# Chunked attention and a gated FFN on one core: weight blocks of 1024 columns, a new plan, and score and value products that take either half of two PSUM banks

## The chip, the cores and the metric

The kernel runs on one NeuronCore of a Trainium2 chip. The metric is device microseconds of one execution; the time of a kernel is the median of its runs. TensorE (PE in the profile) does the matrix products, VectorE (DVE) and ScalarE (ACT) the element-wise work, GpSimd (POOL) some element-wise work on SBUF, and SyncE (SP) issues all DMAs in one queue, in order.

## The reference

```python
q_c, k_c, v_c = (a.reshape(B, H, S // 64, 64, D) for a in (q, k, v))   # B, H, S, D = 8, 8, 576, 64
scores = np.matmul(q_c, k_c.transpose(0, 1, 2, 4, 3)) / np.sqrt(D)
attn = np.exp(scores - scores.max(-1, keepdims=True))
attn = attn / (attn.sum(-1, keepdims=True) + 1e-9)
x = np.matmul(attn, v_c)             # to (B, S, H * D), d_model = 512
h = np.maximum(x @ w_in, 0.0)        # d_ff = 1024
conv_out = sum of conv_w[k] * h shifted by k - 1 along S, k = 0, 1, 2
out = (h / (1 + np.exp(-conv_out))) @ w_out
```

The activations are float32; the weights `w_in`, `conv_w`, `w_out` arrive as float64 and are read as pairs of 32-bit words.

## The kernel before

The 4608 rows of the batch are cut two ways: 36 tiles of 128 rows (two attention chunks of 64 each) for the attention and the output, and 16 units of 288 columns for the FFN, of which each has 8 blocks of 128 features.

**Attention, per tile** (`att`, L436). The first nine tiles load q and k as rows (`load_rows`, L98, two DMAs of 256 KB, into one of six slots), transpose them on TensorE (`t_pe`, L139) and copy them out on ScalarE. The other tiles come in groups of three by `load_group` and `load_part` (L108 to L126), eight parts to a group, two group buffers, and are transposed on VectorE (`t_dve`, L150, from line 153). Then: `scores` (L155, 16 small matmuls, line 163), `s_max` and `s_sub` on VectorE (L173, L177), exp on ScalarE (L182), sum and reciprocal on VectorE, the normalisation on GpSimd (L195), a transpose on TensorE (L202), a copy (L207), `attn_v` (L209, 16 small matmuls, line 215), and the split of x in a high and a low fp32r part, `x_hi` on ScalarE (L239) and `x_lo` on VectorE (L243). v has five buffers. The PSUM tile `sx` is a pair of banks that scores and attn @ v share: scores always write columns 0 to 255 of both banks, attn @ v columns 256 to 511.

**Weights** (`split`, L401). A block of a weight matrix is 128 partitions by 512 float64 numbers. It lands in one of the same six slots and is turned into a high and a low fp32r matrix by steps on VectorE: `w_mask` (L334), `w_rest` (L343), `w_low` (L347), `w_sign` (L352), `w_pow` (L369); `w_bias` (L339) and the copies `w_hi`, `w_lo_copy` (L362, L380) on ScalarE; `w_lo_big` (L377) on GpSimd. In every second block (`hi_pool`) `w_one` (L358) and a product on GpSimd, `w_hi_one` (L365), take the place of `w_sign` and `w_hi`. There are eight blocks of `w_in`, eight of `w_out` and one small one of `conv_w`.

**FFN.** A block of a unit is `mm1` (L246, 12 matmuls of 290 columns on line 252 into one of three `h_ps` banks), then relu and the convolution on ScalarE and VectorE (L258 to L281), whose last step `c_mul` (L281) frees the `h_ps` bank, then `g_hi` (L290, ScalarE) and `g_lo` (L294, GpSimd). `mm2` (L299, line 305) takes three matmuls of 512 columns per tile and feature block, eight of these to an output tile; `o_copy` (L310) takes the result to one of three `o_sb` buffers and `o_store` (L313) to memory.

**What sets the order.** All steps are listed with an engine, a cost, a key and the buffers that they take and free (`step`, L66; `room`, L397). A planner (L595 to L684) lays them out by these costs and by keys that tables shift (`by_step`, `by_chain`, L566 to L583), and the instructions of each engine are then held to that order. A step with `bank="sx"` is planned so that it doesn't run while another engine works in the pair of banks.

Of the kernel before, what the change touches and what calls it, by code (L numbers as in the profile page):

```python
# [30 lines left out]
def attn_ffn(ctx: ExitStack, tc: tile.TileContext, q, k, v, w_in, conv_w, w_out, out):  # L31
    nc = tc.nc
# [14 lines left out]
    NU = 2 * B  # L47
    NAT = 9
# [29 lines left out]
    rebias = const.tile([P, 1], F32, name="rebias")  # L78
    nc.gpsimd.memset(rebias, -896.0 * 2 ** 23)
# [16 lines left out]
    slots = [sp[:, 1024 * i:1024 * i + 1024] for sp in spare for i in range(TG)]  # L96

    def load_rows(st, t):  # L98
        r = slots[st["slot"]].rearrange("p (i c) -> p i c", i=2)
# [39 lines left out]
    def t_pe(st, i):  # L139

        st["tp", i] = tp = ps_h.tile([P, 512], F32, name="h_ps")
        rows = slots[st["slot"]][:, 512 * i:512 * i + 512]
        for g in range(G):
            nc.tensor.transpose(out=tp[:, P * g:P * g + P], in_=rows[:, P * g:P * g + P], identity=ident)  # L144
# [9 lines left out]

    def scores(st):  # L155

        s_ps = sx[:, :, 0:G * C]
# [12 lines left out]
    def s_max(st):  # L170
        st["sv"] = sx[:, :, 0:G * C].rearrange("p u (g j) -> p u g j", j=C)
# [37 lines left out]
    def attn_v(st):  # L209
        x_ps = sx[:, :, G * C:2 * G * C]  # L210
# [97 lines left out]
    def o_copy(st):  # L308
        st["os"] = work3.tile([P, DM], F32, name="o_sb")
# [9 lines left out]
    def w_load(st, src):  # L319
        np_, n, m2 = src.shape  # L320
        t = slots[st["slot"]].bitcast(U32)[0:np_, 0:n * m2].rearrange("p (n m) -> p n m", m=m2)
# [5 lines left out]
    def w_tile(st, name):  # L327
        t = (work3 if name == "o_sb" else work).tile([P, DM], F32, name=name)
# [3 lines left out]
    def w_mask(st):  # L332
        st["T"] = w_tile(st, "o_sb")
# [21 lines left out]
    def w_one(st):  # L355

        st["S"] = w_tile(st, "ws")
        nc.vector.tensor_scalar(out=st["S"].bitcast(U32), in0=st["H"], scalar1=0x80000000, scalar2=0x3F800000,  # L358
                                op0=ALU.bitwise_and, op1=ALU.bitwise_or)

# [3 lines left out]
    def w_hi_one(st, hi):  # L364
        nc.gpsimd.tensor_tensor(out=hi, in0=st["T"], in1=st["S"], op=ALU.mult)  # L365

    def w_pow(st, hi):
        st["E"] = w_tile(st, "we")
        nc.vector.tensor_scalar(  # L369
            out=st["E"].bitcast(U32), in0=(st["T"] if hi is None else hi).bitcast(U32), scalar1=0xFF800000, scalar2=None,  # L370
# [30 lines left out]
    def split(key, t_load, src, hi=None, lo=None, hi_pool=False, lo_pool=False, lag=1.5):  # L401
# [34 lines left out]
    def att(t, key, load_key, exps, writes):  # L436
# [16 lines left out]
        ldv = step("SP", 2.65, load_key + 0.05 if t < 5 else key - 8, load_v, (st, t), [before.get("v")], take=["v"], lag=1.28)  # L453
# [4 lines left out]
        s = step("DVE", 0.68, key, s_sub, (st,), [s], take=["e"], free=["m", "s"], bank="sx")  # L458
# [25 lines left out]
    def block(key, u, f, after):  # L484
# [4 lines left out]
        s = step("ACT", 0.5, key + 2, c_mid, (st, u, f), [s, cw_done], take=["c"])  # L489
# [26 lines left out]
    def wi(n, key, t_load, **kw):  # L516

        ks = slice(2 * (n % 2), 2 * (n % 2) + 2)
        ends = split(key, t_load, src_i[n], wi_h[:, n // 2, ks, :], wi_l[:, n // 2, ks, :], lag=1.5, **kw)
        for f in (n - n % 2, n - n % 2 + 1):  # L520
            wi_done[f] = wi_done.get(f, []) + list(ends)

    def wo(f, key, t_load, **kw):
# [195 lines left out]
```

## Time and profile before

| | us |
|---|---|
| median of 3 runs | 533.53 (531.76 to 535.38) |
| the profiled execution | 533.55 |
| its span, first to last instruction | 531.8 |
| TensorE busy in the span | 500.3 |
| VectorE busy | 364.6 |
| ScalarE busy | 359.4 |
| GpSimd busy | 184.9 |

The profile shows one execution. Busy times are shares of the span; a wait is the idle time of an engine just before an instruction, put down to what released it last. An average over the span says little here, because the first 90 us and the rest have different limits: stretches have to be read apart.

### The profile page before, as it was taken

The numbers are of one execution on the slowest core, as the hardware profiler recorded it, in microseconds if no ns is written. First come the engines' busy times: TensorE is split into PE (matmuls) and PEld (weight loads), VectorE is DVE, ScalarE is ACT, GpSimd is POOL, SyncE is SP. The second block draws the span as 40 slices with busy tenths as digits, with TensorE's granted clock in tenths as the row PEclk, the third lists the DMA queues.
The fourth block names the chain that finished last, engine by engine and source line by source line (L and its number), as shares of the span: only waits on it lengthen the run. The fifth ranks groups of instructions, "written<-read, shape, count | busy, mean of one in ns | idle before, by whom it ended". The sixth has DMA issues, their size and how long they took to land.

```text
span 531.8 us, 12836 instructions
## 1 busy us (share of the span) xinstructions
PE 500.3 (94%) x4921; PEld 437.6 (82%) x4921; DVE 364.6 (69%) x763; ACT 359.4 (68%) x818; POOL 184.9 (35%) x250
## 2 busy tenths in 40 slices
PE   3577889999999999999989999999999999999997
PEld 2467777988889898889878888889889889988975
DVE  6878999848668775866668586869756597554420
ACT  3568898857766868656756868767666578775630
POOL 2346757531423424322413324231334324241320
PEclk9988998999999999999999999999999999999999
DMA  8996581453344555333644643335440020000011
GB/s 207 241 235 179 129 185 39 108 96 62 48 94 90 105 107 105 87 64 64 109 110 87 128 75 62 64 82 110 78 95 24 21 62 2 21 21 21 21 48 52
DMA packets 183266, 47.03 MB, mean 88 GB/s; under 512 B 175500, under 2 KB 175524, under 8 KB 183204
## 3 DMA queue, kind: packets, MB, share of 16 engines
q1 hardware_dynamic: 183204, 46.20, 39.1%
q8 instruction: 39, 0.64, 0.5%
q14 instruction: 23, 0.19, 0.1%
HBM read 36.72 MB, written 9.44 MB: 87 GB/s over the span
## 4 chain that ended last, share of the span: by engine, by line
PE 78%; SPq 7%; DVE 6%; ACT 5%; DMA 3%; issue 1%; POOL 0%; ACTq 0%; DVEq 0%; POOLq 0%
PE o_ps L305 34%; PE h_ps L252 34%; SPq L124 4%; PE sx_ps L215 3%; PE sx_ps L163 3%; PE pt_ps L202 3%; PE h_ps L144 1%; SPq L136 1%; DMA qk<-in_moe_w_in 1%; DMA v<-in_v 1%; ACT c L263 1%; DVE c L267 1%; ACT L278 1%; DVE c L281 1%; DVE c L273 1%
## 5 line engine op out<-in xcount | busy, mean ns | idle before, releaser
L294 POOL TENSOR_TENSOR g_l<-c,g_h 128x288 fp32r<-128x288 f32 (+8 forms) x184 | 113.5, 633 | 231.7 <-ACT g_h L290 221.6
L305 PE MATMUL o_ps<-wo_h,g_h 128*128 128x512 f32 x288 | 116.9, 406 | 0.6 <-ACT wo_h L362 0.6
L305 PE MATMUL o_ps<-wo_l,g_h 128*128 128x512 f32 x288 | 113.9, 395 | 2.3 <-ACT wo_l L380 2.2
L305 PE MATMUL o_ps<-wo_h,g_l 128*128 128x512 f32 x288 | 113.9, 395 | 0.0
L267 DVE SCALAR_TENSOR_TENSOR c<-h_ps,cw,c 128x288 f32<-128x288 f32 (+1 forms) x128 | 65.6, 513 | 62.3 <-ACT c L263 61.4
L252 PE MATMUL h_ps<-x_h,wi_h 128*128 128x290 f32 x512 | 94.1, 307 | 4.5 <-DVE c L281 4.2
L252 PE MATMUL h_ps<-x_l,wi_h 128*128 128x290 f32 x512 | 91.3, 301 | 0.0
L252 PEld LDWEIGHTS h_ps<-x_h,wi_h 128*128 128x128 f32 x512 | 79.8, 192 | 13.8 <-DVE c L281 6.9
L252 PE MATMUL h_ps<-x_h,wi_l 128*128 128x290 f32 x512 | 90.5, 299 | 0.0
L278 ACT ACTIVATE c<-c 128x288 f32<-128x288 f32 x128 | 55.8, 443 | 38.1 <-DVE c L273 37.0
L252 PEld LDWEIGHTS h_ps<-x_l,wi_h 128*128 128x128 f32 x512 | 77.5, 193 | 0.0
L252 PEld LDWEIGHTS h_ps<-x_h,wi_l 128*128 128x128 f32 x512 | 77.2, 192 | 0.0
L281 DVE TENSOR_TENSOR c<-h_ps,c 128x288 f32<-128x288 f32 x128 | 56.9, 452 | 27.6 <-ACT c L278 26.2
L290 ACT CAST g_h<-c 128x288 fp32r<-128x288 f32 (+8 forms) x184 | 59.4, 357 | 19.9 <-DVE c L281 16.0
L258 ACT ACTIVATE h_ps<-h_ps 128x290 f32<-128x290 f32 x128 | 50.9, 398 | 29.6 <-PE h_ps L252 28.9
L263 ACT ACTIVATE c<-h_ps,cw 128x288 f32<-128x288 f32 x128 | 63.8, 500 | 9.9 <-POOL g_l L294 2.2
L273 DVE SCALAR_TENSOR_TENSOR c<-h_ps,cw,c 128x288 f32<-128x288 f32 (+1 forms) x128 | 65.7, 515 | 3.5
L305 PEld LDWEIGHTS o_ps<-wo_h,g_l 128*128 128x128 f32 x288 | 54.2, 188 | 12.4 <-POOL g_l L294 0.2
L305 PEld LDWEIGHTS o_ps<-wo_l,g_h 128*128 128x128 f32 x288 | 54.3, 188 | 11.0 <-ACT wo_l L380 3.2
L305 PEld LDWEIGHTS o_ps<-wo_h,g_h 128*128 128x128 f32 x288 | 54.3, 189 | 10.4 <-ACT wo_h L362 0.8
L195 POOL TENSOR_TENSOR e<-e,z 128x512 f32<-128x512 f32 x36 | 39.3, 1092 | 64.5 <-DVE z L192 56.4
L310 ACT COPY o_sb<-o_ps 128x512 f32<-128x512 f32 x36 | 21.0, 584 | 33.0 <-PE o_ps L305 32.4
(53 smaller groups left out, 536.0 us busy)
## 6 DMA issues: line engine op xcount, KB each, us to landing
v<-in_v SPq DMA_DIRECT2D x144, 64.0 KB, 2.8
out<-o_sb SPq DMA_DIRECT2D x36, 256.0 KB, 2.1
qk<-in_q SPq DMA_DIRECT2D x96, 48.0 KB, 2.4
qk<-in_k SPq DMA_DIRECT2D x96, 48.0 KB, 2.2
qk<-in_moe_w_in SPq DMA_DIRECT2D x8, 512.0 KB, 6.5
qk<-in_moe_w_out SPq DMA_DIRECT2D x8, 512.0 KB, 5.5
qk<-in_q SPq DMA_DIRECT2D x96, 24.0 KB, 1.9
qk<-in_k SPq DMA_DIRECT2D x96, 24.0 KB, 1.9
```

Source lines behind the costliest of these rows:

```text
L124: nc.sync.dma_start(out=groups[j][p0:p0 + 32, i, g, n0:n0 + 2 * n, :], in_=(q, k)[i][b, 2 * g + hp, t0:t0 + C * n, 32 * a:32 * a + 32].rea ...
L195: nc.gpsimd.tensor_tensor(out=st["e"], in0=st["e"], in1=st["z"].rearrange("p (h o) -> p h o", o=1).broadcast_to([P, H, C]), op=ALU.mult)
L252: nc.tensor.matmul(h_ps[:, 0:XU], lhsT=wt[:, f // 2, kt, P * (f % 2):P * (f % 2) + P], rhs=xt[:, u % NX, kt, :], start=n == 0, stop=n == 3 ...
L258: nc.scalar.activation(out=st["h"][:, 0:XU], in_=st["h"][:, 0:XU], func=AF.Relu)
L263: nc.scalar.mul(out=st["c"], in_=st["h"][:, i0:i0 + HS], mul=cw[:, FT + f:FT + f + 1])
L267: nc.vector.scalar_tensor_tensor(out=c[:, a:HS], in0=st["h"][:, i0 + a - 1:i0 + HS - 1], scalar=cw[:, f:f + 1], in1=c[:, a:HS], op0=ALU.mu ...
L273: nc.vector.scalar_tensor_tensor(out=c[:, 0:b], in0=st["h"][:, i0 + 1:i0 + 1 + b], scalar=cw[:, 2 * FT + f:2 * FT + f + 1], in1=c[:, 0:b], ...
L278: nc.scalar.activation(out=st["c"], in_=st["c"], func=AF.Sigmoid)
L281: nc.vector.tensor_tensor(out=st["c"], in0=st["h"][:, st["i0"]:st["i0"] + HS], in1=st["c"], op=ALU.mult)
L290: nc.scalar.copy(out=g_h[:, f, gs], in_=st["c"][:, cs])
L294: nc.gpsimd.tensor_tensor(out=g_l[:, f, gs], in0=st["c"][:, cs], in1=g_h[:, f, gs].bitcast(F32), op=ALU.subtract)
L305: nc.tensor.matmul(st["o"], lhsT=gt[:, f, o:o + P], rhs=wt[:, f, :], start=f == 0 and n == 0, stop=f == FT - 1 and n == 2)
```

## The change

Weights are split in blocks of 1024 numbers per partition (two slots of their own, `w_slots`); only the first two blocks of `w_in` are still split as two halves of 512 each. The variant with `w_one` and `w_hi_one` is gone. Rows of q and k have two slots instead of six, v four buffers instead of five; the output tile and the first weight tile share a pair of buffers `wt`, where the output had three. Scores and attn @ v take whichever half of the pair of banks is free. An exp at the start of the kernel brings ScalarE's table in. Costs of the planner are changed, among them that of a change of TensorE between kinds of matmul, and the two tables of shifts hold other numbers throughout.

```diff
-    rawv = ctx.enter_context(tc.tile_pool(name="rawv", bufs=5))
+    rawv = ctx.enter_context(tc.tile_pool(name="rawv", bufs=4))
+    work1 = ctx.enter_context(tc.tile_pool(name="work1", bufs=1))
...
+    nc.scalar.activation(out=rebias, in_=ident[:, 0:1], func=AF.Exp)
...
-    slots = [sp[:, 1024 * i:1024 * i + 1024] for sp in spare for i in range(TG)]
+    slots = [sp[:, 2048:3072] for sp in spare]
+    w_slots = [sp[:, 0:2048] for sp in spare]
...
+    def sx_half(i):
+        return sx[:, :, G * C * i:G * C * i + G * C]
...
-        s_ps = sx[:, :, 0:G * C]
+        s_ps = sx_half(st["s"])
...
-        x_ps = sx[:, :, G * C:2 * G * C]
+        x_ps = sx_half(st["x"])
...
-        st["os"] = work3.tile([P, DM], F32, name="o_sb")
+        st["os"] = work.tile([P, 2 * DM], F32, name="wt")[:, 0:DM]
...
-    def w_one(st):
-    def w_hi_one(st, hi):
...
-    src_i = [w_in.rearrange("(k p) f -> p k f", p=P)[:, 2 * (n % 2):2 * (n % 2) + 2, 4 * P * (n // 2):4 * P * (n // 2) + 4 * P] for n in range(FT)]
-    src_o = [w_out.rearrange("(k p) f -> p k f", p=P)[:, f:f + 1, :] for f in range(FT)]
-    room = {"slot": 2 * TG, "grp": 2, "v": 5, "qT": 2, "kT": 2, "m": 2, "e": 3, "z": 2, "pT": 2, "c": 4, "o_sb": 3,
-            "wv": 2, "we": 2, "ws": 2, "s": 1, "x": 1, "pt": 1, "h": 3, "o": 2}
+    src_i = [w_in.rearrange("(k p) f -> p k f", p=P)[:, :, 4 * P * n:4 * P * n + 4 * P] for n in range(FT // 2)]
+    src_o = [w_out.rearrange("(k p) f -> p k f", p=P)[:, 2 * n:2 * n + 2, :] for n in range(FT // 2)]
+    room = {"slot": 2, "wslot": 2, "sx": 2, "grp": 2, "v": 4, "qT": 2, "kT": 2, "m": 2, "e": 3, "z": 2, "pT": 2, "c": 4, "wt": 2,
+            "wv": 2, "we": 1, "pt": 1, "h": 3, "o": 2}
...
-        a, b, c, p = (0.2, 0.28, 0.35, 0.4) if small else (0.42, 0.68, 0.62, 1.28)
+        a, b, c, p = (0.2, 0.28, 0.35, 0.4) if small else (0.42, 0.68, 0.62, 1.28) if half else (0.69, 1.22, 1.06, 2.35)
...
-        s = step("PE", 0.47, key, scores, (st,), tt + [before.get("s")], take=["s"], free=["qT", "kT"], bank="sx")
+        s = step("PE", 0.47, key, scores, (st,), tt + [before.get("s")], take=[("sx", st, "s")], free=["qT", "kT"], bank="sx")
...
+        parts = [slice(0, 2), slice(2, 4)] if n in (0, 1, ) else [slice(0, 4)]
...
-        "w_bias": 3, "w_rest": 1.5, "w_sign": 1, "w_pow": -1.5, "w_hi": 5, "w_lo": 2.5, "w_one": 0.5, "w_hi_one": 1,
+        "w_load": 7, "w_mask": -3.5, "w_bias": -4, "w_rest": -3, "w_low": -3.5, "w_pow": -13.5, "c_sum": -27.5, "c_pe":
...
-    f32 = {scores, p_pe, attn_v, t_pe, c_pe}
+    kinds = {scores: 1, attn_v: 1, p_pe: 2, t_pe: 2, c_pe: 2}
+    turn = {(0, 1): (0.07, 0.0), (1, 0): (0.12, 0.1), (1, 2): (0.12, 0.06), (2, 1): (0.07, 0.0)}
```

What the change makes of the order is seen at three places. First, VectorE's queue from its start to the first maximum over scores (`m<-sx_ps`), before:

```order
L334 TENSOR_SCALAR o_sb<-qk 128x512
L358 TENSOR_SCALAR ws<-qk 128x512
L343 TENSOR_SCALAR wv<-qk 128x512
L347 SCALAR_TENSOR_TENSOR wv<-qk,wv 128x512
L334 TENSOR_SCALAR o_sb<-qk 128x512
L343 TENSOR_SCALAR wv<-qk 128x512
L347 SCALAR_TENSOR_TENSOR wv<-qk,wv 128x512
L352 SCALAR_TENSOR_TENSOR o_sb<-qk,o_sb 128x512
L369 TENSOR_SCALAR we<-wi_h 128x512
L369 TENSOR_SCALAR we<-o_sb 128x512
L374 SCALAR_TENSOR_TENSOR wi_l<-wv,we 128x512
L173 TENSOR_REDUCE m<-sx_ps 128x8
```

And VectorE from its start now:

```order
L344 TENSOR_SCALAR wt<-qk 128x512
L353 TENSOR_SCALAR wv<-qk 128x512
L357 SCALAR_TENSOR_TENSOR wv<-qk,wv 128x512
L362 SCALAR_TENSOR_TENSOR wt<-qk,wt 128x512
L370 TENSOR_SCALAR we<-wt 128x512
L344 TENSOR_SCALAR wt<-qk 128x1024
L353 TENSOR_SCALAR wv<-qk 128x1024
L357 SCALAR_TENSOR_TENSOR wv<-qk,wv 128x1024
L362 SCALAR_TENSOR_TENSOR wt<-qk,wt 128x1024
L370 TENSOR_SCALAR we<-wt 128x1024
L183 TENSOR_REDUCE m<-sx_ps 128x8
```

Ahead of the first maximum there stood two blocks of 512, and now a block of 512 and one of 1024, whose load of 1 MB is the second DMA on SP, ahead of the first q and k.

Second, TensorE where attn @ v of tile 2 (`sx_ps<-pT,v`) is followed by the scores of tile 4 and the first `mm1`, with the semaphores that each waits for, before:

```order
L215 MATMUL sx_ps<-pT,v 64x64 [waits DMAHW6_49]
L215 MATMUL sx_ps<-pT,v 64x64 x12
L163 MATMUL sx_ps<-kT,qT 64x64 [waits DVE_49,Activation_49]
L163 MATMUL sx_ps<-kT,qT 64x64 x15
L252 MATMUL h_ps<-x_h,wi_h 128x290 [waits PE_49]
L252 MATMUL h_ps<-x_h,wi_h 128x290 x3
```

The same place on TensorE now:

```order
L225 MATMUL sx_ps<-pT,v 64x64 [waits DMAHW4_49]
L225 MATMUL sx_ps<-pT,v 64x64 x12
L173 MATMUL sx_ps<-kT,qT 64x64 x16
L262 MATMUL h_ps<-x_h,wi_h 128x290 [waits Activation_49]
L262 MATMUL h_ps<-x_h,wi_h 128x290 x3
L262 MATMUL h_ps<-x_l,wi_h 128x290 [waits DVE_49]
```

The scores no longer wait for VectorE there; the wait for x now stands at `mm1`.

Third, the SP queue where the parts of group 7 (tiles 21 to 23, `qk_2926` before, parts of 8 DMAs each) are issued; `qk_3342` is group 8. Before, from the sixth part on:

```order
L124 DMA qk_2926<-in_k 32x6x32 x8
L124 DMA qk_3342<-in_q 32x12x32 x4
L124 DMA qk_3342<-in_k 32x12x32 x4
L124 DMA qk_3342<-in_q 32x12x32 x4
L124 DMA qk_3342<-in_k 32x12x32 x4
L124 DMA qk_3342<-in_q 32x12x32 x4
L124 DMA qk_3342<-in_k 32x12x32 x4
L124 DMA qk_3342<-in_q 32x12x32 x4
L124 DMA qk_3342<-in_k 32x12x32 x4
L313 DMA out_0<-o_sb_3370 128x512
L124 DMA qk_2926<-in_q 32x6x32 x8
L124 DMA qk_2926<-in_k 32x6x32 x8
```

SP at group 7 now (`qk_2989`):

```order
L131 DMA qk_2989<-in_q 32x6x32 x8
L131 DMA qk_2989<-in_k 32x6x32 x8
L131 DMA qk_2989<-in_q 32x6x32 x8
L131 DMA qk_2989<-in_k 32x6x32 x8
L131 DMA qk_2989<-in_q 32x6x32 x8
L131 DMA qk_2989<-in_k 32x6x32 x8
L131 DMA qk_2989<-in_q 32x6x32 x8
L131 DMA qk_2989<-in_k 32x6x32 x8
L143 DMA v_3522<-in_v 64x4x64 x4
L323 DMA out_0<-wt_3255 128x512
L323 DMA out_0<-wt_3504 128x512
```

Before, all eight parts of group 8 went ahead of the last two of group 7; now the eight parts of group 7 stand together, and two output stores stand behind them.

## Rows read from the trace of the kernel before

**Rows 1.** The page's head: busy time, share of the span, instructions.

```profile
span 531.8 us, 12836 instructions
PE 500.3 (94%) x4921; PEld 437.6 (82%) x4921; DVE 364.6 (69%) x763; ACT 359.4 (68%) x818; POOL 184.9 (35%) x250
```

**Rows 2.** Windows: stretch, us; PE, PEld, DVE, ACT, POOL busy; PE clock; DMA share; GB/s.

```profile
30.00:40.00 10.00, 6.39 (x119) 5.54 (x118) 7.05 (x18) 5.88 (x12) 4.14 (x3) 0.85 0.93 266
...
240.00:280.00 40.00, 38.06 (x425) 33.60 (x424) 26.01 (x52) 26.18 (x62) 10.92 (x16) 1.00 0.48 95
...
40.00:90.00 50.00, 42.38 (x400) 36.56 (x401) 46.64 (x101) 43.80 (x94) 34.20 (x29) 0.93 0.56 137
90.00:520.00 430.00, 427.51 (x4180) 376.94 (x4177) 288.42 (x600) 293.64 (x686) 136.38 (x205) 1.00 0.34 71
```

**Rows 3.** TensorE's waits, all and (last) 100 to 520 us: total us, times, longest.

```profile
PE h_ps L252 <- DVE c L281: 4.2, 3, 3.5
...
PE sx_ps L163 <- DVE x_l L243: 1.9, 1, 1.9
PE sx_ps L163 <- DVE kT L153: 1.9, 1, 1.9
...
PE h_ps L252 <- DVE c L281: 0.2, 1, 0.2
```

**Rows 4.** Windows 0 to 105 of tile qk (PE, PEld, DVE), tile we (DVE, POOL), line L365 (POOL).

```profile
0.00:105.00 105.00, 13.93 (x72) 10.35 (x72) 36.63 (x68) 0.95 0.67 163
...
0.00:105.00 105.00, 11.62 (x20) 19.79 (x15) 0.95 0.67 163
...
0.00:105.00 105.00, 12.22 (x8) 0.95 0.67 163
```

**Rows 5.** Timeline: start us, us, engine, line, operation, [idle before <- releaser].

```profile
4.74 0.43 DVE L334 TENSOR_SCALAR o_sb<-qk 128x512 uint32<-128x512 uint32 x1 [4.74 <-DMA qk<-in_moe_w_in]
5.42 0.42 DVE L343 TENSOR_SCALAR wv<-qk 128x512 uint32<-128x512 uint32 x1
5.88 0.69 DVE L347 SCALAR_TENSOR_TENSOR wv<-qk,wv 128x512 f32<-128x512 uint32 x1
9.01 1.11 PE L144 MATMUL h_ps<-ident,qk 128*128 128x128 f32 x4 [0.23 <-DMA qk<-in_k]
12.01 0.69 DVE L173 TENSOR_REDUCE m<-sx_ps 128x8 f32<-128x512 f32 x1
...
37.73 1.33 PE L252 MATMUL h_ps<-x_h,wi_h 128*128 128x290 f32 x4
...
86.56 1.34 DVE L347 SCALAR_TENSOR_TENSOR wv<-qk,wv 128x512 f32<-128x512 uint32 x1
...
127.40 0.50 PE L305 MATMUL o_ps<-wo_h,g_h 128*128 128x512 f32 x1
127.74 0.40 PE L305 MATMUL o_ps<-wo_l,g_h 128*128 128x512 f32 x1
```

**Rows 6.** Groups by line and shape: count, busy us, mean ns, idle before.

```profile
L377 POOL TENSOR_TENSOR wv<-wv,we 128x512 f32<-128x512 f32 x15 | 19.8, 1319 | 15.6 <-DVE we L369 13.7 <-DVE wv L347 1.9
...
L347 DVE SCALAR_TENSOR_TENSOR wv<-qk,wv 24x128 f32<-24x128 uint32 x1 | 0.3, 279 | 0.0
...
L343 DVE TENSOR_SCALAR wv<-qk 24x128 uint32<-24x128 uint32 x1 | 0.2, 206 | 0.0
```

**Rows 7.** Timeline of SP and PE at group 7 of the loads.

```profile
263.94 5.14 SPq L124 DMA_DIRECT2D qk<-in_q  x8
269.13 3.83 SPq L124 DMA_DIRECT2D qk<-in_k  x8
...
270.90 0.40 PE L305 MATMUL o_ps<-wo_h,g_l 128*128 128x512 f32 x1
273.16 0.69 PE L163 MATMUL sx_ps<-kT,qT 64*64 64x64 f32 x32 [1.87 <-DVE kT L153]
```

**Rows 8.** Issues of the SP queue: count, KB each, median us to landing.

```profile
out<-o_sb SPq DMA_DIRECT2D x36, 256.0 KB, 2.1
```

More of the change, by code (lines that the diff above doesn't have):

```diff
@@ L141, in t_pe @@
         st["tp", i] = tp = ps_h.tile([P, 512], F32, name="h_ps")
-        rows = slots[st["slot"]][:, 512 * i:512 * i + 512]
+        rows = row_slot(st)[:, 512 * i:512 * i + 512]
         for g in range(G):
@@ L320, in w_load @@
         np_, n, m2 = src.shape
[L321 removed]
+        t = w_slots[st["wslot"]].bitcast(U32)[0:np_, 0:n * m2].rearrange("p (n m) -> p n m", m=m2)
         nc.sync.dma_start(out=t, in_=src)
@@ L327, in w_tile @@
     def w_tile(st, name):
-        t = (work3 if name == "o_sb" else work).tile([P, DM], F32, name=name)
+        t = (work1 if name == "we" else work).tile([P, 2 * DM], F32, name=name)
         t = t[0:st["p"], 0:st["L"].shape[1] * st["L"].shape[2]]
@@ L467, in att @@
         s = step("ACT", 0.59, key + 12, p_copy, (st,), [s], take=["pT"], free=["pt"])
-        s = step("PE", 0.47, key + 14, attn_v, (st,), [s, ldv], take=["x"], free=["pT", "v"], bank="sx")
+        s = step("PE", 0.47, key + 14, attn_v, (st,), [s, ldv], take=[("sx", st, "x")], free=["pT", "v"], bank="sx")
         n = len(x_views(st, t, x_h)) - 1
         s = step("ACT", 0.58 + 0.15 * n, key + 14, x_hi, (st, t), [s] + writes, bank="sx")
-        return step("DVE", 0.69 + 0.1 * n, key + 14, x_lo, (st, t), [s], free=["x"], bank="sx")
+        return step("DVE", 0.69 + 0.1 * n, key + 14, x_lo, (st, t), [s], free=[("sx", "x")], bank="sx")
     group_loads, before = {}, {}
@@ L516, in wi, with wo @@
     def wi(n, key, t_load, **kw):
[L518 to L523, printed above, removed]
-        wo_done[f] = split(key, t_load, src_o[f], wo_h[:, f:f + 1, :], wo_l[:, f:f + 1, :], **kw)
-    wi(0, 4, 0.0)
-    for f in range(1, FT):
-        wi(f, 4.0 + 4.2 * f, 0.2 + 0.25 * f, hi_pool=f % 2 == 1, lo_pool=True)
-    cw_done = split(16.0, 0.85, src_c)
-    for f in range(FT):
-        wo(f, U[1] - 6 + 4.0 * f, 5.0 + f, hi_pool=f % 2 == 1, lo_pool=True)
+        parts = [slice(0, 2), slice(2, 4)] if n in (0, 1, ) else [slice(0, 4)]
+        wi_done[2 * n] = wi_done[2 * n + 1] = [
+            end for i, ks in enumerate(parts)
+            for end in split(key + 2 * i, t_load + 0.1 * i, src_i[n][:, ks], wi_h[:, n, ks, :], wi_l[:, n, ks, :], half=len(parts) > 1, **kw)]
+    def wo(n, key, t_load, **kw):
+        wo_done[2 * n] = wo_done[2 * n + 1] = split(key, t_load, src_o[n], wo_h[:, 2 * n:2 * n + 2, :], wo_l[:, 2 * n:2 * n + 2, :], **kw)
+    LP = "11111111"
+    cw_done = split(8.0, 0.15, src_c)
+    for n in range(FT // 2):
+        wi(n, 4.0 + 8.4 * n, 0.2 + 0.6 * n, lo_pool=LP[n] == "1")
+    for n in range(FT // 2):
+        wo(n, U[1] - 6 + 8.0 * n, 5.0 + 2 * n, lo_pool=LP[4 + n] == "1")
     exps = {}
@@ L604, in attn_ffn @@
     free_at = dict.fromkeys(early, 0.0)
-    free_at["SP"] = 0.7
+    free_at.update(SP=0.7, ACT=3.0)
     port, other, share = {"DVE": 0.0, "POOL": 0.0}, {"DVE": "POOL", "POOL": "DVE"}, {"DVE": 0.2, "POOL": 0.137}
-    dma_free, table, pe_f32, bank = 0.0, None, False, {}
+    dma_free, table, kind, bank = 0.0, "exp", 0, {}
     left = [len(a) for a in befores]
@@ L635, in attn_ffn @@
                             t = max(t, until_ + late[e])
-                    if e == "ACT" and (table is None or s["table"] not in (None, table)):
+                    if e == "ACT" and s["table"] not in (None, table):
                         t += 1.28
-                    if e == "PE" and (s["fn"] in f32) != pe_f32:
-                        t += 0.12
-                    elif e == "PE" and pe_f32:
-                        key -= 6.0
+                    if e == "PE":
+                        t += turn.get((kind, kinds.get(s["fn"], 0)), (0.0, 0.0))[0]
+                        key -= 6.0 if kind == kinds.get(s["fn"], 0) == 1 else 0.0
                     picks.append((t, key, i))
@@ L651, in attn_ffn @@
         if e == "ACT":
-            table = s["table"] or table or "exp"
+            table = s["table"] or table
         if e == "PE":
-            if pe_f32 and s["fn"] not in f32:
-                cost += 0.1
-            pe_f32 = s["fn"] in f32
+            cost += turn.get((kind, kinds.get(s["fn"], 0)), (0.0, 0.0))[1]
+            kind = kinds.get(s["fn"], 0)
         if s["port"]:
```

87 lines of the change are left out of this document (40 added, 47 removed), and 18 rows, old and new, of the table by_chain.

## The prediction

> **What bounds the kernel now.** I read the head of the page first: TensorE is busy 500.3 of 531.8 us [rows 1], so the time is its work plus what it waits. Then the windows, to see where it waits. From 90 to 520 us it is busy 427.5 of 430; from 40 to 90 us only 42.4 of 50, and from 30 to 40 us 6.4 of 10 [rows 2]. The reader is to see two regimes. In the steady part nothing but TensorE's own work counts, save one window, 240 to 280 us, with 1.9 us idle. In the start it is VectorE that is full: 46.6 of 50 us from 40 to 90 [rows 2], because the weights are split there while the first tiles and units want it too. The granted clock is 0.85 on the mean in the idle stretch from 30 us, between its two levels of 1.2 and 2.4 GHz, and 1.00, the upper one, after 90 us; it fell where TensorE stood, so I don't price it by itself. Third, the list of TensorE's waits: 4.2 us for `c_mul` (a full `h_ps` bank, which is VectorE being late), 1.9 us of scores behind `x_lo`, and 1.9 us of scores behind a transposed k [rows 3]. The last is the idle of the window from 240 us: TensorE stands from the end of a matmul at 270.9 to 273.16 because k of group 7 was not there, and SP was still issuing that group's last two parts at 263.94 and 269.13 [rows 7]. So there are two places to gain, the start and group 7. The total work of TensorE can't fall: the count of its matmuls is the same before and after.
>
> **The weights on VectorE.** Before, the splits take it 36.6 us (everything that reads `qk` up to 105 us) and 11.6 us (what touches `we`), together 48.3 us [rows 4]. With GpSimd idle, a tensor_scalar on 512 columns takes 0.42 us and a scalar_tensor_tensor 0.69 [rows 5]. Eight blocks with mask, rest, pow as the first kind and low, sign as the second, eight with mask, rest, one, pow and low, and one `w_lo`, make 56 x 0.42 + 25 x 0.69 = 40.8, and some 1.7 for the small block: 42.5. The other 5.8 us is slowing beside GpSimd, seen in one row of 1.34 us against 0.69 [rows 5].
>
> The new width is not in the trace. On 128 columns the two kinds take 0.21 and 0.28 us [rows 6], so a column costs (0.42 - 0.21) / 384 = 0.00055 and (0.69 - 0.28) / 384 = 0.00107 us, and 1024 columns 0.42 + 0.28 = 0.70 and 0.69 + 0.55 = 1.24. Bounds: twice the 512 (0.84, 1.38), were nothing fixed in it, and 0.42 + 0.21 and 0.69 + 0.41 (the whole 128-column time fixed, and half the saving again). A full block is then 3 x 0.70 + 2 x 1.24 = 4.6 us (4.1 to 5.3), and all of it 4 halves x 2.64 + 6 x 4.6 + 1.7 = 39.9: 2.6 less than 42.5, with 1.5 more to 5.6 less as the ends. I take the middle value, as it rests on two rows of the same operations. GpSimd's share of the splits falls from 19.8 + 12.2 = 32.0 us [rows 4] to 4 x 1.32 + 6 x 2.64 = 21.1 at most [rows 6]; if the slowing goes with it, 5.8 x 11/32 = 2.0 us less. So VectorE is freed of 4.6 us by the time that the weights are done. ScalarE gets what GpSimd loses, four products of `w_out` and four of `w_in`, but copies of 1024 have one fixed part instead of two; I price it at 0, covered by its 6.2 us of idle from 40 to 90 us [rows 2].
>
> **The start of it.** Before, the second block of 512 and the first k had landed at 9.01 us, after 1.56 MB; the first maximum over scores stood at 12.01 [rows 5]. Now 1.5 MB of weights come first, so the big block lands near 9.0, and its 4.6 us stand ahead of the first maximum: 13.6, which is 1.6 later. VectorE has the first half done at 4.74 + 2.64 = 7.4 and waits the 1.6 us to 9.0, idle that it did not have. The exp table, now loaded while the DMA runs, is worth nothing here for that reason: VectorE waits for the load anyway. The wait of 1.9 us behind `x_lo` ahead of the first `mm1` (at 37.73 [rows 5]) goes, as the order shows, and `x_hi` now waits 0.65 us for the scores instead; since VectorE is the one that is full, I don't count the difference.
>
> The Trainium skill (PSUM — Partial Sum Buffer, section PSUM bank collisions raise a hardware error ⚠️) says that two engines may not work in one bank and quadrant at once, whatever the columns. The row of 1.9 us agrees: scores waited for a read of the other half. By that rule the free choice of a half gives no overlap of engines, only other turns, which is how I count it; were the halves independent, `x_hi` would not wait either, and the sum would be 0.65 us lower.
>
> So the start gives 4.6 - 1.6 = 3.0 us, if TensorE gains what VectorE is freed of. Ends: none at all, and 7.6 us, all of TensorE's idle from 40 to 90 us [rows 2].
>
> **The steady part.** The parts of group 7 now stand together, and the eight parts of group 8 that stood ahead of the last two are gone from there. TensorE's 1.9 us [rows 7] go; what is late next in that stretch is nothing that the list of waits shows (one wait of 0.2 us from 100 to 520 us besides [rows 3]). Ends: 0 if another wait stands there, 1.9. In the new order TensorE changes between the three kinds of matmul 157 times against 154. After scores the first matmul takes 0.50 us and the next 0.40 [rows 5], so 3 x 0.1 = 0.3 us more (0 to 1). ScalarE loads its tables 30 times against 28, hidden by its idle after 90 us (294 of 430 busy [rows 2]).
>
> The buffers taken away I price at 0. One v less and two slots for rows hold a load back at the start only where VectorE is late to free them, which the VectorE count above has in it. Two output buffers instead of three: the copy of a tile waits until the tile two earlier has been stored. A tile takes at least 24 matmuls of 0.231, 5.55 us, so two tiles 11.1, and a store lands in 2.1 [rows 8]: 9.0 us of cover, while SP holds a store back. If that cover is gone ScalarE stands, with relu of the next block behind it, and TensorE with it.
>
> **Sum**, against the profiled execution of 533.55 us (span 531.8 and 1.75 around it; the median of the runs is the same within 0.02): 533.55 - 3.0 - 1.9 + 0.3 = 528.95, say 529.0.
>
> **Rivals.**
> A. The slowing and the idle both go. VectorE falls behind only because its steps are stretched beside GpSimd and find blocks late; with 11 us less on GpSimd the whole idle of 40 to 90 us goes, 7.6 us: 533.55 - 7.6 - 1.9 + 0.3 = 524.4. For it: VectorE's longest step there is twice its length alone. Against it: VectorE is 93% busy there, and a freed 4.6 us can't fill 7.6. The Trainium skill (SBUF — State Buffer, section Who interferes with whom) says that a VectorE instruction with two SBUF inputs contends with a GpSimd instruction that reads SBUF. By that the low and sign steps are those that gain, and the row of 1.34 us is one; it raises this rival's chance, though there remain 20 such steps, 12 of them long.
>
> B. The start gives nothing. The order has VectorE do as much before tile 6's `x_lo` as before (its steps up to there, counted in the two orders at the same durations, make 84 us against 83), as it draws the big blocks forward; then only group 7 counts: 533.55 - 1.9 + 0.3 = 532.0. For it, that sum and the 1.6 us of the start. Against it, by then the weights are all done, where before one block was left, and slowing is not in the sum.
>
> C. Slower: output stores behind group loads. In the new SP order a store stands behind four parts of group 4 and two behind all eight of group 7. Four parts of 3.83 us [rows 7] hold a store 15.3 us, 6.3 beyond the 9.0 of cover if output tiles come at their densest. Then ScalarE and TensorE stand 6.3 us, at two places 12.6: 533.55 - 4.6 + 12.6 = 541.6. One such stall alone decides, since it costs more than the 4.6 gained: from a store held 13.6 us at the densest spacing. Against it: 36 tiles in 430 us come 12 us apart on the mean, and two tiles are then 24 us.
>
> **How the numbers follow.** Chances: the forecast 0.46, A 0.20, B 0.22, C 0.12. A measurement of this kernel tells about 1% from no change, 528.2 to 538.9. A lies below, as does the lower third of the forecast's own range (526.5 to 531.5): 0.20 + 0.17, and a little for widths cheaper than I took, 0.38. C makes slower 0.10, with its single stall (533.55 - 4.6 + 6.3 = 535.3) in the same class. Same: 0.52. The range leaves out the tail of A and the two-stall half of C: 523.5 to 536.0.
>
> **What would show it.** Right: instructions of VectorE on 1024 columns near 0.70 and 1.24 us; the first maximum over scores near 13.6; VectorE's sum for the splits near 44; idle of TensorE from 40 to 90 us near 5 instead of 7.6; no wait for k near 270 us. Wrong: waits of ScalarE's output copy for a DMA (C), a first `mm1` after 38 us with the old idle after it (B), TensorE full from 45 us on (A).

## The result, and the profile after

The changed kernel takes 528.05 us (median of 4 runs, 526.54 to 528.57) against 533.28 for the kernel before, a ratio of 0.9898 with a 95% interval of 0.9867 to 0.9928: 5.2 us, 1.0% faster. The prediction was 529.0. The sum came out nearly right by luck: two of its three terms were wrong, and their errors cancelled. The rest is about that.

The head of the page after [rows 1]:

```profile
span 526.6 us, 12790 instructions
PE 496.3 (94%) x4921; PEld 438.0 (83%) x4921; DVE 356.2 (68%) x732; ACT 363.6 (69%) x812; POOL 170.7 (32%) x237
```

The windows after, in the columns of [rows 2]:

```profile
30.00:40.00 10.00, 8.34 (x120) 7.28 (x121) 6.68 (x17) 5.03 (x11) 2.32 (x2) 0.55 1.07 252
40.00:90.00 50.00, 41.00 (x384) 35.56 (x382) 46.30 (x82) 42.84 (x80) 25.32 (x19) 0.93 0.53 140
90.00:520.00 430.00, 429.63 (x4210) 381.53 (x4209) 282.10 (x594) 296.35 (x691) 133.72 (x203) 1.00 0.34 72
240.00:280.00 40.00, 40.00 (x457) 35.48 (x459) 29.91 (x62) 27.61 (x64) 11.50 (x16) 1.00 0.42 89
```

The idle at group 7 is gone (40.00 of 40). But from 40 to 90 us TensorE is busy 41.0 us, less than the 42.4 of before, where the prediction wanted 45. TensorE's largest wait up to 110 us, after the one for the first load, against [rows 3]:

```profile
PE h_ps L262 <- DVE c L291: 4.5, 4, 3.7
```

Busy times mislead here: a matmul's modelled end overlaps the next one's start, so short waits count as busy, and so does a matmul at the lower clock. What shows where the time went is a ledger: time gone less work done, at the start of each run of equal matmuls in TensorE's rows. The work is the known sequence of steps at unit prices that a fit to the rows from 95 to 515 us gives (0.542 us for four matmuls of `mm1`, 0.231 for one of `mm2`, 0.515 for scores or attn @ v of a tile, 0.27 for four transposes; 459.7 us in all, the same in both kernels). Lost time up to a point, us:

| point, us | before | after | gain in the stretch |
|---|---|---|---|
| 37.8 (first `mm1`) | 29.86 | 29.94 | -0.1 |
| 95 | 47.78 | 48.43 | -0.6 |
| 260 | 54.75 | 55.34 | 0.1 |
| 275 (group 7) | 57.79 | 56.27 | 2.1 |
| 500 | 67.99 | 62.78 | 3.7 |

In this pair of traces, then, the start gave nothing, group 7 gave its 2.1 us, and 3.7 us came from 275 us on, where the prediction had a loss of 0.3. The steady part repeats from trace to trace: from 275 to 500 us 9.7 to 10.2 us are lost in three kernels with the old order there (the one before and two of the experiments below, e5 and e9), 6.4 to 6.9 in seven with the new one. The start repeats less well, as is told below beside e3 and e4.

The durations at the new width were right. VectorE's first rows after, against [rows 5]:

```profile
8.23 1.54 DVE L344 TENSOR_SCALAR wt<-qk 128x1024 uint32<-128x1024 uint32 x1 [0.36 <-DMA qk<-in_moe_w_in]
9.69 0.68 DVE L353 TENSOR_SCALAR wv<-qk 128x1024 uint32<-128x1024 uint32 x1
10.41 1.23 DVE L357 SCALAR_TENSOR_TENSOR wv<-qk,wv 128x1024 f32<-128x1024 uint32 x1
12.88 0.69 DVE L370 TENSOR_SCALAR we<-wt 128x1024 uint32<-128x1024 uint32 x1
13.64 0.69 DVE L183 TENSOR_REDUCE m<-sx_ps 128x8 f32<-128x512 f32 x1
```

The two kinds take 0.68 and 1.23 us against 0.70 and 1.24 forecast. The first maximum stands at 13.64 us against 13.6, but by two misses that cancel: the big block is there at 8.23 and not at 9.0 us, so that VectorE waits 0.36 us and not 1.6, and its first step takes 1.54 us and not 0.70, most of it beside a product on GpSimd (7.96 to 9.22 us). The sums of the splits up to 105 us (tile `qk`: PE, PEld, DVE; tile `we`: DVE, POOL), against [rows 4]:

```profile
0.00:105.00 105.00, 15.07 (x72) 11.35 (x72) 35.72 (x44) 0.90 0.64 158
...
0.00:105.00 105.00, 6.86 (x13) 19.61 (x10) 0.90 0.64 158
```

VectorE is freed of 48.3 - 42.6 = 5.7 us, more than the 4.6 of the sum. That none of it reached the end has to be explained.

### The profile page after: what moved, and what is told of

It is laid out like the page before. It is cut to its first block, busy times and chain, and to the rows that moved or that the text cites. A ratio compares the mean times of both kernels' runs of the same rounds, so it can differ in the third digit from the quotient of the medians.

```text
span 526.6 us, 12790 instructions
## 1 busy us (share of the span) xinstructions
PE 496.3 (94%) x4921; PEld 438.0 (83%) x4921; DVE 356.2 (68%) x732; ACT 363.6 (69%) x812; POOL 170.7 (32%) x237
## 4 chain that ended last, share of the span: by engine, by line
PE 87%; DVE 8%; ACT 2%; DMA 1%; issue 1%; POOL 0%; SPq 0%; DVEq 0%; POOLq 0%; ACTq 0%
PE o_ps L315 37%; PE h_ps L262 37%; PE sx_ps L225 4%; PE sx_ps L173 4%; PE pt_ps L212 3%; PE h_ps L151 2%; DMA qk<-in_q 1%; DVE wv L357 1%; DVE c L277 1%; DVE wt L362 1%; DVE c L283 1%; DVE z L196 1%; DVE c L291 1%; DVE we L370 1%; DVE e L187 0%
## 5 line engine op out<-in xcount | busy, mean ns | idle before, releaser
L277 DVE SCALAR_TENSOR_TENSOR c<-h_ps,cw,c 128x287 f32<-128x287 f32 (+1 forms) x128 | 65.4, 512 | 69.0 <-ACT c L273 68.6
L283 DVE SCALAR_TENSOR_TENSOR c<-h_ps,cw,c 128x288 f32<-128x288 f32 (+1 forms) x128 | 65.6, 514 | 3.0
L205 POOL TENSOR_TENSOR e<-e,z 128x512 f32<-128x512 f32 x36 | 37.9, 1067 | 64.6 <-DVE z L202 54.1
L320 ACT COPY wt<-o_ps 128x512 f32<-128x512 f32 x36 | 21.1, 585 | 24.5 <-PE o_ps L315 23.9
```

The costliest lines, as they stand in the source:

```text
L205: nc.gpsimd.tensor_tensor(out=st["e"], in0=st["e"], in1=st["z"].rearrange("p (h o) -> p h o", o=1).broadcast_to([P, H, C]), op=ALU.mult)
L277: nc.vector.scalar_tensor_tensor(out=c[:, a:HS], in0=st["h"][:, i0 + a - 1:i0 + HS - 1], scalar=cw[:, f:f + 1], in1=c[:, a:HS], op0=ALU.mu ...
L283: nc.vector.scalar_tensor_tensor(out=c[:, 0:b], in0=st["h"][:, i0 + 1:i0 + 1 + b], scalar=cw[:, 2 * FT + f:2 * FT + f + 1], in1=c[:, 0:b], ...
L320: nc.scalar.copy(out=st["os"], in_=st["o"])
```

## The experiments

Theory V is the prediction's (VectorE's sum sets the start), theory N the ledger's (the start gives nothing, the gain comes later). The rows of the clock added a third, K: TensorE's lower clock sets the start. The runs go by the numbers in their labels, e1 to e11.

**Group 7 alone, in the kernel before.** The edit to the plan, ahead of the loop that issues the steps:

```diff
+    first8 = min(begin[i] for i in order_ if steps[i]["fn"] is load_part and steps[i]["args"][0] == 8)
+    for i in order_:
+        if steps[i]["fn"] is load_part and steps[i]["args"][0] == 7 and begin[i] > first8:
+            begin[i] = first8 - 1e-3 + 1e-6 * i
```

Expected of e1_group7_first: 

> The kernel before, with the last two parts of group 7 issued ahead of group 8's eight parts and nothing else moved. Two theories of where the change's 5.2 us come from. V (the prediction's): about 3 at the start, because VectorE is freed of work there, and 1.9 at group 7. N (from the two traces): TensorE's lost time (time gone less work done) at 95 us is 0.65 us larger after than before, so the start gives nothing; 2.1 come at group 7 and 3.7 after 275 us. Both say that this edit gives what group 7 gives and no more: 533.3 - 2.0 = 531.3 us, no wait for k near 270 us. If another wait stands behind that one, 533.3.

Measured: 536.18 us, ratio 1.0044 (1.0013 to 1.0076): 2.7 us longer. The wait for k was gone, and this stood in its place (waits of ScalarE and of TensorE, then SP's timeline):

```profile
ACT o_sb L310 <- DMA out<-o_sb: 7.1, 1, 7.1
...
PE sx_ps L215 <- ACT h_ps L258: 3.9, 1, 3.9
```

```profile
272.79 0.41 SPq L313 DMA_DIRECT2D out<-o_sb  x1
```

The store that SP had issued at 263.48 us in the kernel before now stood behind all eight parts of group 8; ScalarE's copy of an output tile waited 7.1 us for the buffer, and TensorE 3.9 us behind ScalarE, after which its matmuls ran at the lower clock for some 6 us (four of `mm1` in 1.17 us in place of 0.70, up to 285 us). This is the mechanism of rival C, in a kernel where the edit had made it. The second try moves the store as well, right behind the two parts:

```diff
...
+    for i in stores:
+        begin[i] = first8 - 0.0005
```

Expected of e5_group7_and_store: 

> The kernel before, with the last two parts of group 7 and the output store that stood ahead of them both issued ahead of group 8's eight parts. In e1_group7_first that store was left behind all eight parts, and ScalarE's copy of an output tile waited 7.1 us for its buffer. N and V: the wait for k goes and no other comes, 533.4 - 2.0 = 531.4 us. Rival: the loads as such are too late in that stretch, whatever their order, and a wait of 1 to 4 us comes at another place: 532.5 to 536.

Measured: 531.25 us against 533.63, ratio 0.9949 (0.9925 to 0.9974), 2.4 us less. Group 7's place in SP's queue is worth what the prediction said, if the store keeps its place too.

**The pairs on TensorE.** In the changed order twelve times two tiles' scores, or two tiles' attn @ v, stand back to back on TensorE; before, none did, as both wrote the same columns. They were taken apart, with the other engines' orders held:

```diff
...
+        if steps[i]["fn"] is steps[j]["fn"] and steps[i]["fn"] in (scores, attn_v) and steps[m]["fn"] in (mm1, mm2):
+            begin[j], begin[m] = begin[m] + 0.001, begin[j]
```

Expected of e2_pairs_apart: 

> The changed kernel, where TensorE's twelve pairs of scores with scores or attn @ v with attn @ v of two tiles, which stand back to back, are taken apart by the mm1 or mm2 step behind them; all else stays. N: the gain after 275 us is to a large part that such a pair costs one change to the small matmuls and back (0.15 us over its work) where two single ones cost 0.20 to 0.22 each: 12 x 0.26 = 3.1 us longer, 531.2. If the pairs are worth nothing and the gain comes from other waits: 528.1 +- 0.5. V says nothing of them: 528.1.

Measured: 538.43 us, ratio 1.0078 (1.0056 to 1.0099), some 10 us longer than the changed kernel. One such place in TensorE's timeline of the changed kernel:

```profile
135.23 0.39 PE L315 MATMUL o_ps<-wo_h,g_l 128*128 128x512 f32 x1
135.55 1.16 PE L173 MATMUL sx_ps<-kT,qT 64*64 64x64 f32 x64
136.64 0.50 PE L315 MATMUL o_ps<-wo_h,g_h 128*128 128x512 f32 x1
136.97 0.39 PE L315 MATMUL o_ps<-wo_l,g_h 128*128 128x512 f32 x1
```

And of the kernel with the pairs apart:

```profile
134.15 0.39 PE L315 MATMUL o_ps<-wo_h,g_l 128*128 128x512 f32 x1
134.47 0.69 PE L173 MATMUL sx_ps<-kT,qT 64*64 64x64 f32 x32
135.10 0.50 PE L315 MATMUL o_ps<-wo_h,g_h 128*128 128x512 f32 x1
135.43 0.39 PE L315 MATMUL o_ps<-wo_l,g_h 128*128 128x512 f32 x1
```

From the start of the last `mm2` matmul ahead to that of the second one behind, a pair takes 136.97 - 135.23 = 1.74 us and a single tile 1.28. Without the two `mm2` matmuls (0.46) that is 1.28 for two tiles against 0.82 for one: two single ones cost 0.36 us more than a pair. Put another way, a stand of such products costs 0.36 us beyond 0.46 for each tile in it, whether one tile stands in it or two. Over the whole stretch from 95 to 505 us the ledger has 4.6 us for the twelve, 0.38 each, more than the 0.26 expected. Most of the other 5.7 us is waits: ScalarE's wait for attn @ v rose from 4.4 to 13.0 us, as its order was held while the product came later. So this run prices a pair, but doesn't show by its total what the change had from it.

**Fixed halves, planned anew.**

```diff
-    room = {..., "sx": 2, ...}
+    room = {..., "s": 1, "x": 1, ...}
...
-        s_ps = sx_half(st["s"])
+        s_ps = sx_half(0)
...
-        x_ps = sx_half(st["x"])
+        x_ps = sx_half(1)
...
```

Expected of e6_one_half: 

> The changed kernel with scores bound to the first half of the pair of banks and attn @ v to the second, as before the change; the plan is made anew with the same costs, keys and tables (so its order differs throughout). N: no pairs of scores with scores can stand in the plan, and TensorE's time over its work from 95 to 505 us rises from 14.3 us by 2 to 6: 530 to 534. If the free half is worth nothing by itself and the new costs and tables give all: 528 +- 1.5.

Measured: 541.49 us, ratio 1.0130 (1.0076 to 1.0184). Lost time from 95 to 505 us is 23.4 us against 14.3. Of these 9.1, 29 single tiles in place of 7 single ones and 12 pairs make 4.7 (10.0 us against 5.3, counted from the last large matmul ahead to the second behind, as above), gaps inside the large products 2.4. The rest, like the 1.7 us more at 95 us, comes with an order that the tables of shifts were not made for, and is no price of the half.

**Less and more work for VectorE, same order.** In e3 `w_low` is left out for blocks of 1024; in e4 `w_rest` is done twice for them.

```diff
     def w_low(st):
+        if st["L"].shape[1] * st["L"].shape[2] == 1024:
+            return
```

Expected of e3_less_vector: 

> The changed kernel without the step w_low in the six blocks of 1024 (the low words of these weights are left out of the computation): VectorE has 6 x 1.22 = 7.3 us less to do before 95 us, in the same order. V: the start ends with VectorE's sum, so 4 to 7 us less: 521 to 524. N: TensorE's start is not set by VectorE's sum but by waits that this does not touch; 526.5 to 528.5, and TensorE's lost time at 95 us falls by less than 1.6.

Expected of e4_more_vector: 

> The changed kernel with w_rest done twice in the six blocks of 1024 (the second writes the same values): VectorE has 6 x 0.70 = 4.2 us more to do before 95 us, in the same order. V: about 4 us longer, 532. N: 0 to 1.5 us longer, 528 to 529.5.

Measured: 526.40 us (ratio 0.9852, 0.9812 to 0.9892) and 530.75 (0.9939, 0.9918 to 0.9961): 1.65 less for 7.3 us of work taken away, 2.7 more for 4.2 added. Both theories missed: VectorE's time counts, but by the medians only a quarter to two thirds of it.

The ledger at 95 us moved by -2.3 and +1.8 against the changed kernel's trace, but a single trace doesn't tell the start that finely. Of the kernels with the old order and work up to there, e1 has lost 0.9 us less than the kernel before and e5 0.7 more; of those with the new one, e8 (below) has lost 0.6 less than the changed kernel and e2, whose order differs only from 99.9 us on, 1.9 less. The means of these three and three traces lie 0.1 us apart, the changed start being the shorter. So the start gave no gain that can be told from zero, and against the mean e3 moved by -1.5 and e4 by +2.6, as the medians did.

Where work was taken away, VectorE waited instead: for ScalarE's steps of the convolution 6.6 us from 38 to 95 us (e3), against 3.3.

**The table's preload taken out.**

```diff
-    nc.scalar.activation(out=rebias, in_=ident[:, 0:1], func=AF.Exp)
```

Expected of e8_no_preload: 

> The changed kernel without the exp at its start, so that ScalarE brings its table in at its first use, in the same order otherwise. V and N, as in the prediction: nothing, 527.5 to 528.6, since VectorE waits for the 1 MB block until about 8.2 us anyway. Rival: the table then stands in the chain of the first block (mask, bias, sign): up to 1.3 us longer, 529.4.

Measured: 528.11 us (ratio 0.9878, 0.9837 to 0.9918): nothing that can be told from the changed kernel's 528.05, as the prediction had it.

**TensorE's gaps filled.** At the start TensorE runs at the lower of its clock's levels (1.2 GHz) for long stretches: four matmuls of `mm1` take 1.17 us there and 0.70 at the upper. The changed kernel's timeline:

```profile
37.92 1.32 PE L262 MATMUL h_ps<-x_h,wi_h 128*128 128x290 f32 x4 [0.39 <-ACT x_h L249]
...
47.28 1.34 PE L262 MATMUL h_ps<-x_h,wi_h 128*128 128x290 f32 x4 [3.72 <-DVE c L291]
...
51.31 1.17 PE L262 MATMUL h_ps<-x_l,wi_h 128*128 128x290 f32 x4
```

After the wait of 3.72 us the rows stay at 1.17 until 52.3 us; in the kernel before they were back at 0.70 from 50.65. Useless transposes were put in the gaps:

```diff
+    fill = {0: 18, 2: 2, 5: 3, 6: 3, 10: 3, 11: 4, 12: 6, 15: 4, 20: 3, 22: 2, 25: 26, 29: 8}
...
+            for _ in range(fill.get(n_pe, 0)):
+                junk = junk or ps_o.tile([P, 512], F32, name="o_ps")
+                nc.tensor.transpose(out=junk[:, 0:P], in_=ident, identity=ident)
...
```

Expected of e7_filled_start: 

> The changed kernel with 82 transposes of the unit matrix into an unused bank, put into TensorE's gaps up to 57 us (18 ahead of the first tile, 26 ahead of the fourth mm1, 2 to 8 at ten other places). In the changed kernel matmuls at the lower clock take some 12 us longer up to 53 us than the same would at the upper. K (the clock of the start sets its length): with the gaps filled the clock stays up from about 15 us on, first mm1 earlier than 37.9 by 2 to 4 us, total 523 to 526. Rival: the first 50 us are set by loads, VectorE and ScalarE, and TensorE's slow matmuls stand beside them: 527.5 to 529, or up to 2 us longer where the filling delays real work.

Measured: 525.15 us (ratio 0.9836, 0.9789 to 0.9882), 2.9 less than the changed kernel by the medians, and the shortest of all that compute everything; its interval overlaps the changed kernel's by a little, so against that one the gain rests on the ledger too, which at 95 us has 3.1 less than the changed kernel's trace and 1.3 less than the lowest of the three with this start. A window and the timeline:

```profile
30.00:40.00 10.00, 8.73 (x144) 7.59 (x145) 8.21 (x20) 6.23 (x14) 2.33 (x2) 1.00 1.08 261
```

```profile
35.36 0.80 PE L262 MATMUL h_ps<-x_h,wi_h 128*128 128x290 f32 x4
...
40.91 3.00 PE L684 MATMUL o_ps<-ident 128*128 128x128 f32 x26
...
45.70 0.81 PE L262 MATMUL h_ps<-x_h,wi_h 128*128 128x290 f32 x4 [1.79 <-DVE c L291]
```

The first `mm1` comes 2.6 us earlier, at the upper clock (1.00 from 30 to 40 us, where it was 0.55). Part of this is chance in the changed kernel's trace: the same order ran at 1.00 there without any filling in e2, where the first `mm1` stood at 36.16 us:

```profile
36.16 0.80 PE L262 MATMUL h_ps<-x_h,wi_h 128*128 128x290 f32 x4 [0.39 <-ACT x_h L249]
```

Without the last two fillings (`25: 26, 29: 8` taken out), expected of e11_filled_early: 

> e7_filled_start without its last two fillings (26 ahead of the fourth mm1, 8 ahead of a later attn @ v). If the early part of the clock counts: first mm1 at 35.4 as there, then rows of 1.2 to 1.3 us at the fourth mm1 again, and 1 to 2 us of the 2.9 remain: 526 to 527. If only the fourth mm1 counts: 528.

Measured: 526.63 us (ratio 0.9867, 0.9836 to 0.9899): half of the gain by the medians, with an interval that overlaps both that of e7 and that of the changed kernel. Its trace is of its shortest execution, 525.24 us: there the lower clock is back at 45.5 to 49.8 us, and yet the ledger has only 0.2 more at 95 us than e7. So the share of the last two fillings stays open.

The same filling in the kernel before (83 transposes at its own gaps), expected of e9_before_filled: 

> The kernel before, with 83 such transposes in TensorE's gaps up to its fourth mm1, placed as in e7_filled_start. There the changed kernel became 2.9 us shorter, all of it ahead of 95 us, so the lower clock was on the path. Open is why VectorE's 5.7 us less gave nothing at 95 us. K: the changed kernel's lower clock (from 26.5 to 39 and 47.3 to 52.6 us, before 36.8 to 40.5 and 47.6 to 50.6) ate the gain; with the clock up in both, TensorE's lost time at 95 us is 1.5 to 4 us less for the changed kernel than here, so 531.5 to 533.5 here. Rival W: the order of the changed start is itself no shorter, and the fill gives the same here: 530 to 531, lost time at 95 us 45 as in e7_filled_start.

Measured: 531.22 us against 533.40, ratio 0.9963 (0.9945 to 0.9981), 2.2 less. Its timeline:

```profile
36.42 0.80 PE L252 MATMUL h_ps<-x_h,wi_h 128*128 128x290 f32 x4
...
46.36 0.80 PE L252 MATMUL h_ps<-x_h,wi_h 128*128 128x290 f32 x4 [1.96 <-DVE c L281]
```

Lost time at 95 us is 45.88 here and 45.30 in e7. With the clock up in both from about 18 us on, the changed start is 0.6 us shorter; without the filling it is 0.6 longer by the two traces and 0.1 shorter by the means. So of what VectorE was freed of the clock ate about 1 us, where K expected 1.5 to 4. This lies nearer to W: the order of the changed start is itself hardly shorter.

Last, e7 without `w_low` in the large blocks, expected of e10_filled_less_vector: 

> e7_filled_start without w_low in the six blocks of 1024 (the low words of these weights are left out), 7.3 us less for VectorE. With the clock low this gave 1.65 us (e3_less_vector). K: with the clock up VectorE sets the start, and more of it counts: 3 to 6 us less than e7_filled_start, 519 to 522. Rival: the same third of it as before, 1.5 to 2.5 us less: 522.7 to 523.6.

Measured: 523.57 us (0.9816, 0.9777 to 0.9855), by the medians 1.6 less than e7, a quarter of 7.3 us again. But the two intervals overlap widely, and the trace, taken of the longest of four executions (525.98 us), doesn't decide it: the granted clock was down again there (0.83 from 20 to 30 and 0.72 from 47 to 53 us), and lost time at 95 us is 1.0 more than in e7. That all of the 7.3 us count is ruled out; whether more of them count with the clock up than in e3 stays open.

## Why the prediction was right in its sum and wrong in its steps

**The start (forecast -3.0, measured +0.6 in this pair of traces, -0.1 by the means of three).** The step that failed is "So the start gives 4.6 - 1.6 = 3.0 us, if TensorE gains what VectorE is freed of". The first number was larger than forecast (5.7 us freed), the second came out by the two misses named above (1.6 later); the condition did not hold. Where the 5.7 us were freed shows in the same two sums cut into three stretches, tile `qk` and then tile `we`, before:

```profile
0.00:38.00 38.00, 9.56 (x40) 6.92 (x40) 14.43 (x30) 0.99 0.89 227
38.00:95.00 57.00, 4.37 (x32) 3.43 (x32) 20.58 (x35) 0.92 0.56 134
95.00:110.00 15.00, 0.00 (x0) 0.00 (x0) 1.62 (x4) 1.00 0.54 110
...
0.00:38.00 38.00, 5.42 (x9) 5.30 (x4) 0.99 0.89 227
38.00:95.00 57.00, 5.79 (x10) 13.21 (x10) 0.92 0.56 134
95.00:110.00 15.00, 0.41 (x1) 1.27 (x1) 1.00 0.54 110
```

And after:

```profile
0.00:38.00 38.00, 10.28 (x40) 7.71 (x40) 13.88 (x24) 0.83 0.90 218
38.00:95.00 57.00, 3.54 (x24) 2.65 (x24) 21.84 (x20) 0.93 0.53 133
95.00:110.00 15.00, 1.26 (x9) 0.99 (x8) 0.00 (x0) 1.00 0.39 77
...
0.00:38.00 38.00, 3.18 (x8) 6.94 (x5) 0.83 0.90 218
38.00:95.00 57.00, 3.69 (x5) 10.91 (x6) 0.93 0.53 133
```

Up to 38 us VectorE splits for 17.1 us instead of 19.9, from 38 to 95 for 25.5 instead of 26.4, and behind 95 for 0 instead of 2.0. The 2.0 were work that TensorE didn't wait for (the only wait that its list has from 85 to 110 us, before, is 0.3 us for ScalarE's copy of a k), now drawn forward. The 2.8 ahead of 38 us lie where VectorE itself waits, 8.4 us before and 9.9 after, for its first weights and for scores above all, and TensorE's first `mm1` came at 37.92 against 37.73. In the stretch where VectorE is full it was freed of 0.8 us. This is the mechanism of rival B, which had the right sum for it (84 against 83 us up to tile 6's `x_lo`); the argument against it, that by then the weights are all done, names the very work that moved forward. The chain of the changed kernel from 38 to 90 us is mostly VectorE's:

```profile
by line: PE h_ps L262 18.2%; DVE wv L357 9.4%; DVE c L277 8.7%; DVE c L283 7.4%; DVE wt L362 6.6%; DVE c L291 5.0%; DVE wt L344 4.6%; DVE we L370 4.0%; DVE wv L353 3.9%; DVE e L187 3.8%; DVE m L183 3.5%; DVE z L196 3.4%; DVE x_l L253 2.9%; 
```

Yet e3 and e4 gave a quarter to two thirds of what was taken or added: the chain goes back and forth between VectorE, ScalarE and TensorE, and in e3 VectorE's waits for ScalarE grew by 3.3 us as its own work shrank. That this is why so little of the freed time counts is argued from where it lies, and not shown by a run of its own. A row of 93% busy was no proof that an engine's time counts in full.

**Group 7 (forecast -1.9, measured -2.1).** Right in mechanism and size; e5 alone gave 2.4, e1 showed that the store's place belongs to it.

**The steady part (forecast +0.3, measured -3.7).** The step that failed is "TensorE changes between the three kinds of matmul 157 times against 154 ... so 3 x 0.1 = 0.3 us more". It counted the changes and gave them one price, 0.1 us, read from the first large matmul behind; a stand of small products costs 0.36 in all, by e2. The other half of the step, that besides group 7 "nothing but TensorE's own work counts", failed too.

The ledger from 275 to 505 us, with each stand counted as in e2, puts 1.7 us of the gain into the small products and transposes and 2.0 into the large products. Of scores and attn @ v 30 tiles stood in 21 places there before, and 29 stand in 17 now (57 in 41 and 58 in 36 from 95 us on), while the changes grew by transposes that stand alone. Four places fewer at 0.36 make 1.4 us.

Inside the large products gaps of 0.08 to 0.35 us come to 1.7 us before and to nothing after. All but one of 0.2 us [rows 3] are too short to stand in the list of waits, but the rows show what ended four of them, 1.1 us in all (1.5 with the slower matmul that follows each): `mm1` starts as VectorE's `c_mul` frees its `h_ps` bank. One of them, before, VectorE's row first:

```profile
438.20 0.45 DVE L281 TENSOR_TENSOR c<-h_ps,c 128x288 f32<-128x288 f32 x1
...
438.20 0.40 PE L305 MATMUL o_ps<-wo_h,g_l 128*128 128x512 f32 x1
438.70 0.82 PE L252 MATMUL h_ps<-x_h,wi_h 128*128 128x290 f32 x4
```

The next start is 0.50 us away where 0.23 is the work, and 0.05 behind the end of `c_mul`. The other traces with the old order (e5, e9) have three or four such waits as well, the changed kernel, e3, e7 and e8 have none. Places and waits make 2.9 of the 3.7 us. Which part of the new plan removed the waits, and what makes the rest, no run here took apart.

The prediction took the free half as giving "only other turns" and priced that at nothing. The Trainium skill (PSUM — Partial Sum Buffer, section PSUM bank collisions raise a hardware error ⚠️) says that no two engines may be in one bank and quadrant at once, and in the traces of both kernels no two engines ever work on `sx` at the same time. But two tiles' scores need no second engine: they stand in the bank together before VectorE reads either, and a pair of them costs 0.36 us less than two single ones (e2).

**The terms priced at 0.** The preload is worth nothing (e8). The smaller pools cost nothing that a wait shows: no copy of an output tile waits for a DMA in the changed kernel. Rival A's 524.4 did not come: the slowing beside GpSimd fell (the splits' 42.6 us are 2.7 over the 39.9 forecast for them alone, where they were 5.8 over 42.5), but the idle of 40 to 90 us grew to 9.0. Nor does the slowing keep to the steps that the prediction named, low and sign: the longest step of the first big block is the mask, which has one input in SBUF and took 1.54 us where others like it take 0.69.

## What to carry to other kernels

Work taken from a busy engine counts only where it lies in the stretch that the engine bounds; cut its sum at the first and the last wait that matter before it goes into a forecast. Where TensorE hardly idles, compare two orders by lost time step by step, with a price for each stand of small products, since neither busy time nor the list of waits shows such losses. Before a ledger of one trace is trusted in a stretch, look at how far other traces with the same order lie apart there: here 0.5 us in the steady part and up to 1.9 in the start. A queue's order is repaired together with what stands between the moved items: here a store left behind cost more than the repaired loads gave.

## What the runs showed of the hardware

Filling TensorE's gaps in the first 53 us with 82 useless transposes made the changed kernel 2.9 us shorter by the medians, and, with 83, the kernel before 2.2: work whose results nobody uses paid for itself, because from about 18 us on the matmuls behind the gaps ran at 2.4 instead of 1.2 GHz (0.80 against 1.32 us for the first four of the first `mm1`).

The clock of the start is not the same in each execution of one order: from 30 to 40 us the granted clock was 0.55 in the changed kernel's trace and 1.00 in that of e2, whose order up to there is the same, and by 95 us the two are 1.9 us apart.

The profile page's row of the granted clock is not to be trusted in the first 20 us: it shows 1.00 there in both kernels, while four transposes take 1.1 us, which take 0.66 later at the upper level.

A change of TensorE to small matmuls (64x64, fp32) and back cost 0.36 us in a full queue, whether one tile's 32 stood there or two tiles' 64 (e2).
